# Delta rule and FFN in one kernel: chunks of 64 tokens over four batches in step, with block inverses on VectorE

## The chip, the cores and the metric

The kernel runs on one core of one Trainium2 chip. The metric is device time in microseconds, from one launch of the whole kernel; before the change it is 1528.0 us, the median of three runs (1525.26 to 1528.27). The engines go by these names: PE is TensorE's matrix products, PEld its weight loads, DVE is VectorE, ACT is ScalarE, POOL is GpSimd, and SP is the engine whose queue issues most of the DMAs.

## The reference

Two blocks follow each other. The first is a delta rule over 768 tokens for each of 4 batches and 8 heads, with a head size of 48. For each head a state of 48 x 48 is kept:

```python
k_n = k / (norm(k) + 1e-06)
for t in range(S):
    y[t]  = q[t] @ state
    v_old = k_n[t] @ state
    state = state + beta[t] * outer(k_n[t], v[t] - v_old)
```

The heads' outputs, side by side, make x with 3072 rows of 384. The second block is an FFN in which two products are multiplied with each other:

```python
a = x @ w1            # 384 -> 1024
b = x @ w2            # 384 -> 1024
out = (a * b @ w3) @ w_out   # 1024 -> 1024 -> 384
```

The weights come in float64, the rest in float32.

## The kernel before

Within a chunk of C tokens the delta rule is a triangular system. With S the state before the chunk and A strictly lower, A[t, s] = beta_s (k_t . k_s), the kernel solves (I + A) Z = V - K S, and then y = Q S + tril(Q K^T diag(beta), -1) Z and S' = S + (beta K)^T Z.

Chunks have 128 tokens of one batch. There are 24 steps, 6 chunks for each of 4 batches, and two batches alternate, so that the steps of one pair of batches are done before those of the other. For each step, `scores` does what does not wait for the state: TensorE transposes keys and queries (L261), multiplies them (L275), VectorE applies beta and the triangle (L283), and then the inverses of the diagonal blocks of 32 rows are built by doubling the block size from 2 to 32. Each doubling masks A on POOL (L295), and runs two or three groups of four products with all heads of the group on 128 x 128 (L304), with a copy on ACT (L323) and subtractions on VectorE (L328) between them. `chain` is what the state goes through: V - K S (L366, L371), Z by the block inverse (L375), three passes that settle the blocks below the diagonal (L379, L382), the output (L388, L393), the new state (L401, L415), and transposes of y so that features are on partitions (L426).

The FFN works on 384 tokens of a batch at a time. w3 and w_out are multiplied with each other once (`fold`, L505), so that it has three products per token block: two into a and b (`ab`, L449), and one with the folded weight (`o`, L463). Weights are loaded as float64 words and rounded to float32 by seven VectorE operations and one on POOL (`load_weight`, L145 to L168).

The order of the work is the order in which instructions are written, for each engine by itself. `together` (L512) takes turns between the chain of step i and the scores of step i+1, and after every second turn it emits one unit of the list `units`: first weights, then the parts of the FFN as their tokens come ready. DMAs are issued by SP in the order of the program (a DMA that has to wait holds those behind it), and the output by ACT.

Of the kernel before, what the change touches and what calls it, by code (L numbers as in the profile page):

```python
# [8 lines left out]
FP32 = mybir.dt.float32  # L9
U32 = mybir.dt.uint32  # L10
ALU = mybir.AluOpType
AX = mybir.AxisListType
# [12 lines left out]
# The FFN is ((x w1) * (x w2)) (w3 w_out): nothing stands between w3 and w_out.  # L25
# [3 lines left out]
def kernel(  # L29
# [14 lines left out]
    P = 128  # L44
    C = 128
    BS = 32
    LEVELS = [4, 8, 16, 32]
    DM = H * D
    DF = moe_w3.shape[0]
    BH = B * H  # L50
    NP = H // 2
    NCH = S // C
    KM = DM // P
    KF = DF // P
    CT = 3
    NT = CT * C
    assert S % NT == 0 and NT == DM and D == 48 and H == 8 and B % 2 == 0 and LEVELS[-1] == BS
# [3 lines left out]
    stage = ctx.enter_context(tc.tile_pool(name="stage", bufs=3))  # L61
# [3 lines left out]
    psW = ctx.enter_context(tc.tile_pool(name="psW", bufs=5, space=bass.MemoryType.PSUM))  # L65
    psY = ctx.enter_context(tc.tile_pool(name="psY", bufs=1, space=bass.MemoryType.PSUM))
    psF = ctx.enter_context(tc.tile_pool(name="psF", bufs=2, space=bass.MemoryType.PSUM))

    def bank(pool, tag):
        return pool.tile([P, 512], FP32, tag=tag, name=f"ps_{tag}")  # L70

    def quad(ps):
        return ps.rearrange("p (x w) -> p x w", x=4)

# [1 line left out]
    ident = const.tile([P, P], FP32, name="ident")  # L76
    make_identity(nc, ident[:])
    strict = const.tile([P, P], FP32, name="strict")
# [4 lines left out]
    )  # L83

    def same_block(n):
        t = work.tile([P, P // n, n], FP32, tag="same", name=f"same{n}")
        nc.gpsimd.memset(t[:], 1.0)
        nc.gpsimd.affine_select(
            out=t[:], in_=t[:], pattern=[[-n, P // n], [0, n]], compare_op=ALU.is_ge,
            fill=0.0, base=0, channel_multiplier=1,  # L90
        )
        nc.gpsimd.affine_select(
            out=t[:], in_=t[:], pattern=[[n, P // n], [0, n]], compare_op=ALU.is_ge,
            fill=0.0, base=n - 1, channel_multiplier=-1,
        )
        return t[:].rearrange("p a b -> p (a b)")

    masks = {}
    lower = ident[:]
    for n in [2] + LEVELS:  # L100
        upper = same_block(n)
        masks[n] = const.tile([P, P], FP32, name=f"mask{n}")
        nc.vector.tensor_tensor(out=masks[n][:], in0=upper, in1=lower, op=ALU.subtract)
        lower = upper
    masks["off"] = const.tile([P, P], FP32, name="mask_off")
    nc.vector.tensor_scalar(
        out=masks["off"][:], in0=lower, scalar1=-1.0, scalar2=1.0, op0=ALU.mult, op1=ALU.add
    )

    def four(m):  # L110
        return m[:].unsqueeze(1).to_broadcast([P, 4, P])

# [1 line left out]
    kbufs, bkbufs, qbufs = [], [], []  # L114
    for lst, nm, cnt in ((kbufs, "kb", 2), (qbufs, "qb", 2), (bkbufs, "bkb", 2)):
        for i in range(cnt):
            t = persist.tile([P, NP, 2, 64], FP32, name=f"{nm}{i}")
            nc.gpsimd.memset(t[:, :, :, D:64], 0.0)
            lst.append(t)
    states = []  # L120
    for b in range(B):
        t = persist.tile([P, NP, 2 * D], FP32, name=f"state{b}")
        nc.gpsimd.memset(t[:], 0.0)
        states.append(t)
    beta_tok = persist.tile([P, NCH, BH], FP32, name="beta_tok")

# [1 line left out]
    CW = 256  # L128

    def load_weight(dst, src):  # L130
        if src.dtype == FP32:
            nc.sync.dma_start(out=dst, in_=src)
            return
        n = src.shape[1]
        raw = stage.tile([P, CW, 2], U32, tag="raw", name="raw", bufs=2)
        nc.sync.dma_start(
            out=raw[:, 0:n].rearrange("p n w -> p (n w)"), in_=src.bitcast(U32)
        )
        lo, hi = raw[:, 0:n, 0], raw[:, 0:n, 1]
        sgn = work.tile([P, CW], U32, tag="wa", name="wa", bufs=2)  # L140
        man = work.tile([P, CW], U32, tag="wb", name="wb", bufs=2)
        s, m = sgn[:, 0:n], man[:, 0:n]
        sf, mf = s.bitcast(FP32), m.bitcast(FP32)
        # +-2^exponent: 0 below float32's normal range, infinite above it
        nc.vector.tensor_scalar(  # L145
            out=s, in0=hi, scalar1=20, scalar2=0x7FF,
            op0=ALU.logical_shift_right, op1=ALU.bitwise_and,
        )
        nc.vector.tensor_scalar(
            out=s, in0=s, scalar1=896.0, scalar2=1151.0, op0=ALU.max, op1=ALU.min  # L150
        )
        nc.vector.tensor_scalar(
            out=s, in0=s, scalar1=896.0, scalar2=8388608.0, op0=ALU.subtract, op1=ALU.mult
        )
        nc.vector.scalar_tensor_tensor(
            out=s, in0=hi, scalar=0x80000000, in1=s, op0=ALU.bitwise_and, op1=ALU.bitwise_or
        )
        # 1.mantissa
        nc.vector.tensor_scalar(
            out=m, in0=hi, scalar1=0xFFFFF, scalar2=None, op0=ALU.bitwise_and  # L160
        )
        nc.vector.tensor_scalar(
            out=mf, in0=m, scalar1=2.0**-20, scalar2=1.0, op0=ALU.mult, op1=ALU.add
        )
        nc.vector.scalar_tensor_tensor(
            out=mf, in0=lo, scalar=2.0**-52, in1=mf, op0=ALU.mult, op1=ALU.add
        )
        nc.gpsimd.tensor_tensor(out=dst, in0=mf, in1=sf, op=ALU.mult)  # L168

    w1s = const.tile([P, KM, DF], FP32, name="w1s")  # L170
    w2s = const.tile([P, KM, DF], FP32, name="w2s")
    w34 = const.tile([P, KF, DM], FP32, name="w34")

# [1 line left out]
    GN = 4  # L175
    steps = [(g * 2 + i, c) for g in range(B // 2) for c in range(NCH) for i in range(2)]
    N = len(steps)
    kfs, qfs, vfs, invs, Ps, Fs = {}, {}, {}, {}, {}, {}

    def chunk(src, i):  # L180
        b, c = steps[i]
        return src[b, :, c * C : (c + 1) * C, :].rearrange("h t d -> t h d")

    def load_k(g):
        kfs[g] = stage.tile([P, GN, H, D], FP32, tag="kf", name="kf", bufs=2)
        for j in range(GN):
            nc.sync.dma_start(out=kfs[g][:, j], in_=chunk(k, g * GN + j))

    def load_qv(i):
        for lst, nm, src in ((qfs, "qf", q), (vfs, "vf", v)):  # L190
            lst[i] = stage.tile([P, H, D], FP32, tag=nm, name=nm, bufs=3)
            nc.sync.dma_start(out=lst[i][:], in_=chunk(src, i))

# [1 line left out]
    def norms(g):  # L195
        ss = small.tile([P, GN, H], FP32, name="ss")
        for j in range(GN):
            sq = work.tile([P, H, D], FP32, name="sq", bufs=1)
            nc.vector.tensor_tensor(out=sq[:], in0=kfs[g][:, j], in1=kfs[g][:, j], op=ALU.mult)
            nc.vector.tensor_reduce(out=ss[:, j, :], in_=sq[:], axis=AX.X, op=ALU.add)  # L200
        seed = small.tile([P, GN, H], U32, name="seed")
        nc.vector.tensor_scalar(
            out=seed[:], in0=ss[:].bitcast(U32), scalar1=-0.5, scalar2=1597463007.0,
            op0=ALU.mult, op1=ALU.add,
        )
        r = seed[:].bitcast(FP32)
        for _ in range(3):
            t = small.tile([P, GN, H], FP32, name="nt", bufs=3)
            nc.vector.scalar_tensor_tensor(
                out=t[:], in0=ss[:], scalar=-0.5, in1=r, op0=ALU.mult, op1=ALU.mult  # L210
            )
            nc.vector.tensor_tensor(out=t[:], in0=t[:], in1=r, op=ALU.mult)
            rn = small.tile([P, GN, H], FP32, name="nr", bufs=3)
# [377 lines left out]
```

## Time and profile before

| what | before |
|---|---|
| median of three runs | 1528.0 us (1525.26 to 1528.27) |
| span of the profiled execution | 1523.8 us |
| instructions in it | 23891 |
| PE busy | 1442.6 us, 95% |
| DVE busy | 670.2 us, 44% |
| POOL busy | 546.6 us, 36% |
| ACT busy | 269.6 us, 18% |
| moved by DMA | 38.33 MB, 25 GB/s over the span |
| mean granted TensorE clock | 0.970 |

The span is from the first to the last instruction of one profiled execution; it lies 4.2 us under the median of the timed runs. "Busy" is the time in which an engine had an instruction under way. Matrix products are pipelined, so a busy PE is not a PE at its peak. A row of a group reads: line, engine, operation, what is written from what, shapes, count, then busy microseconds and the mean nanoseconds of one, and after the second bar the idle time just before them with what ended it. A row of the timeline reads: start, length, engine, line, operation, count. A row of a stretch reads: the stretch, its length, then busy time and count for PE, PEld, DVE, ACT and POOL, then the granted clock (1 is full), the busy share of the 16 DMA engines, and GB/s. An issue row ends with the kilobytes of one DMA and the microseconds from its issue to its landing.

### The profile page before, as it was taken

Reading aid. Unit: us, or ns where it says so; the run is one execution under the profiler, and the core shown is the slowest. Engines: PE = TensorE matmul, PEld = TensorE weight load, DVE = VectorE, ACT = ScalarE, POOL = GpSimd, SP = SyncE. Lnnn points to the kernel's source line nnn. Section 1 sums busy time; section 2 is a strip of 40 time slices with the busy share of each in tenths; the row PEclk is TensorE's granted clock in tenths of the full one; section 3 lists DMA queues with packets and bytes.
Section 4 is the critical chain, followed back from the end, with each engine's and each line's share of the span. In section 5 each row is a group of like instructions: output and inputs, shape, how many; then the busy total and the mean of one; then the engine's idle time right before and its main releaser. Section 6 shows DMA issues by size and latency. Waiting matters only on the chain.

```text
span 1523.8 us, 23891 instructions
## 1 busy us (share of the span) xinstructions
PE 1442.6 (95%) x9966; PEld 1246.7 (82%) x9966; DVE 670.2 (44%) x1422; ACT 269.6 (18%) x513; POOL 546.6 (36%) x489
## 2 busy tenths in 40 slices
PE   4888979999999989999999999999999999999999
PEld 3886868999988878888888888888888898889755
DVE  7998967886323343233263233332333232332100
ACT  1121202112211211121112112111121111111111
POOL 7655454655243142241342331431431422413000
PEclk8898989988999989999999999999999999999999
DMA  5221212220000000000010000000000000000000
GB/s 106 74 66 63 85 48 78 59 67 25 12 1 11 18 25 17 1 11 16 11 27 11 12 22 12 1 12 16 11 6 1 17 12 1 1 6 11 1 16 16
DMA packets 88907, 38.33 MB, mean 25 GB/s; under 512 B 76448, under 2 KB 81632, under 8 KB 88800
## 3 DMA queue, kind: packets, MB, share of 16 engines
q1 hardware_dynamic: 85248, 31.99, 8.5%
q10 hardware_dynamic: 3552, 4.82, 0.9%
q8 instruction: 79, 1.29, 0.4%
q14 instruction: 28, 0.23, 0.1%
HBM read 32.08 MB, written 4.72 MB: 24 GB/s over the span
## 4 chain that ended last, share of the span: by engine, by line
PE 74%; POOL 12%; DVE 10%; issue 1%; DMA 1%; ACT 0%; POOLq 0%; DVEq 0%
PE ps_w L304 28%; PE ps_w L352 15%; PE ps_f L449 13%; PE ps_f L463 6%; POOL M L295 6%; POOL W L312 3%; DVE AQ L283 3%; POOL offoff L295 3%; PE ps_y L393 3%; PE ps_f L505 2%; PE ps_w L275 2%; PE ps_w L261 1%; PE ps_w L401 1%; PE ps_w L366 1%; DMA raw<-in_moe_w_dram 1%
## 5 line engine op out<-in xcount | busy, mean ns | idle before, releaser
L295 POOL TENSOR_TENSOR M<-AQ,mask 128x512 f32<-128x512 f32 x240 | 313.8, 1326 | 526.4 <-PE ps_w L304 429.2
L304 PE MATMUL ps_w<-T,M 128*128 128x128 f32 x1536 | 211.3, 292 | 18.7 <-POOL M L295 15.3
L304 PEld LDWEIGHTS ps_w<-T,M 128*128 128x128 f32 x1536 | 194.2, 204 | 23.1 <-POOL M L295 19.3
L304 PE MATMUL ps_w<-W,X 128*128 128x128 f32 x1536 | 202.3, 277 | 0.0
L456 DVE TENSOR_TENSOR ab<-a,ps_f 128x384 f32<-128x384 f32 x64 | 35.5, 554 | 355.1 <-PE ps_f L449 355.1
L304 PEld LDWEIGHTS ps_w<-W,X 128*128 128x128 f32 x1536 | 186.5, 193 | 0.8
L328 DVE TENSOR_TENSOR W<-W,ps_w 128x512 f32<-128x512 f32 x192 | 131.6, 685 | 71.2 <-PE ps_w L304 71.0
L352 PE MATMUL ps_w<-E,W 128*128 128x48 f32 x1152 | 144.8, 281 | 16.4 <-DVE E L379 16.4
L304 PE MATMUL ps_w<-X,W 128*128 128x128 f32 x1152 | 159.0, 282 | 0.0
L352 PEld LDWEIGHTS ps_w<-E,W 128*128 128x128 f32 x1152 | 143.3, 202 | 18.2 <-DVE E L379 17.1
L352 PEld LDWEIGHTS ps_w<-Z,offoff 128*128 128x128 f32 x1152 | 142.4, 195 | 17.0 <-issue 1.3
L304 PEld LDWEIGHTS ps_w<-X,W 128*128 128x128 f32 x1152 | 143.3, 196 | 0.0
L352 PE MATMUL ps_w<-Z,offoff 128*128 128x48 f32 x1152 | 139.1, 274 | 0.0
L449 PE MATMUL ps_f<-xT,w1s 128*128 128x384 f32 x384 | 137.0, 491 | 0.0
L323 ACT COPY X<-ps_w 128x512 f32<-128x512 f32 x192 | 112.6, 587 | 136.3 <-PE ps_w L304 136.3
L449 PE MATMUL ps_f<-xT,w2s 128*128 128x384 f32 x384 | 134.3, 486 | 0.0
L382 ACT COPY Z<-ps_w 128x384 f32<-128x384 f32 x72 | 34.5, 479 | 559.0 <-PE ps_w L352 559.0
L463 PE MATMUL ps_f<-w,ab 128*128 128x384 f32 x384 | 128.6, 490 | 0.0
L328 DVE TENSOR_TENSOR T<-T,ps_w 128x512 f32<-128x512 f32 x144 | 98.8, 686 | 50.5 <-PE ps_w L304 47.7
L449 PEld LDWEIGHTS ps_f<-xT,w2s 128*128 128x128 f32 x384 | 73.0, 190 | 50.9
L463 PEld LDWEIGHTS ps_f<-w,ab 128*128 128x128 f32 x384 | 72.1, 192 | 48.3 <-issue 2.5
L379 DVE TENSOR_TENSOR E<-R,ps_w 128x384 f32<-128x384 f32 x60 | 33.1, 552 | 158.5 <-PE ps_w L352 158.5
(91 smaller groups left out, 1495.4 us busy)
## 6 DMA issues: line engine op xcount, KB each, us to landing
raw<-in_moe_w_dram SPq DMA_DIRECT2D x56, 256.0 KB, 3.1
kf<-in_k_dram SPq DMA_DIRECT2D x24, 192.0 KB, 3.8
qf<-in_q_dram SPq DMA_DIRECT2D x24, 192.0 KB, 3.2
vf<-in_v_dram SPq DMA_DIRECT2D x24, 192.0 KB, 2.7
out_dram<-osb ACTq DMA_DIRECT2D x24, 192.0 KB, 1.8
raw<-in_moe_w_out_dram SPq DMA_DIRECT2D x16, 192.0 KB, 2.3
beta_fm<-in_beta_dram ACTq DMA_DIRECT2D x2, 48.0 KB, 3.2
```

Of the source, the lines that this page charges most:

```text
L283: nc.vector.scalar_tensor_tensor(out=AQ[:, 2 * e + pp], in0=ps[:, 256 * pp : 256 * pp + 256].rearrange("p (j w) -> p j w", j=2), scalar=be ...
L295: nc.gpsimd.tensor_tensor(out=t[:], in0=AT, in1=four(masks[n]), op=ALU.mult)
L304: nc.tensor.matmul(quad(ps)[:, x, :], lhsT=lhs[:, x, :], rhs=rhs[:, x, :], start=True, stop=True)
L312: nc.gpsimd.tensor_tensor(out=W[:], in0=four(ident), in1=M[:], op=ALU.subtract)
L323: nc.scalar.copy(out=X[:], in_=ps)
L328: nc.vector.tensor_tensor(out=t[:], in0=t[:], in1=ps, op=ALU.subtract)
L352: nc.tensor.matmul(ps[:, D * h : D * h + D], lhsT=of_head(tiles, h), rhs=Z[:, D * h : D * h + D], start=True, stop=True,)
L382: nc.scalar.copy(out=Z[:], in_=per_head(F["W"], E))
L393: nc.tensor.matmul(py[:, D * h : D * h + D], lhsT=of_head(F["AQ"], h)[:, 1, :], rhs=Z[:, D * h : D * h + D], start=(c == 0), stop=True, sk ...
L449: nc.tensor.matmul(ps[:, 0:NT], lhsT=w[:, m, js], rhs=cur["x"][:, m, :], start=(m == 0), stop=(m == KM - 1),)
L456: nc.vector.tensor_tensor(out=cur["ab"][jc][:], in0=a[:], in1=pair[1][:, 0:NT], op=ALU.mult)
L463: nc.tensor.matmul(ps[:, 0:DM], lhsT=cur["ab"][jc][:, ts * P : (ts + 1) * P], rhs=w34[:, jc, :], start=(jc == 0), stop=(jc == KF - 1),)
```

## The change

The delta rule and its staging are written anew; the FFN keeps its products. A is kept without beta and without normalised keys: with n the norms of the keys and w = beta / n^2, the solution is scaled instead of the operands.

- A chunk has 64 tokens, and all four batches go through a chunk together: two batches lie on partitions 0 to 63 and 64 to 127 (index z), two such pairs lie side by side (index r). There are 12 chunks. Products use 64-row and 64-column parts of TensorE's array, one for each z.
- Keys and queries are loaded a second time, in blocks of 32 tokens by 32 features (`load_perm`, 32 DMAs per chunk), so that VectorE's transpose of 32 x 32 blocks brings features onto partitions (`prep`).
- The diagonal blocks of 32 rows of two chunks (128 blocks) are written to DRAM and read back with one block per partition (`to_blocks`, `inverse`). VectorE inverts all 128 at once, row by row: 31 times a product and a subtraction. They go back by DRAM into their places (`from_blocks`).
- `corner` makes the one block below the diagonal blocks out of two products, so that the whole inverse of 64 rows is there and `chain` needs one product by it, with no passes.
- `chain` gets y with features on partitions straight out of the products; ACT copies it into the FFN's input, and six small DMAs fill the remaining rows. The FFN works on 512 tokens at a time (two chunks of four batches).
- `load_weight` rounds 512 columns at a time with two operations on ACT, two on VectorE and one on POOL.
- The order is written out: per chunk `chain`, then the next chunk's `corner`, then on even chunks the preparation and the inverse of the two chunks after, then six units.

Of the diff, the lines of the new functions; what they replace is in the kernel above, and the norms, the fold and the masks change in small ways only:

```diff
-    C = 128
+    C = 64
     BS = 32
...
+    psW = ctx.enter_context(tc.tile_pool(name="psW", bufs=2, space=bass.MemoryType.PSUM))
+    psT = ctx.enter_context(tc.tile_pool(name="psT", bufs=1, space=bass.MemoryType.PSUM))
+    psF = ctx.enter_context(tc.tile_pool(name="psF", bufs=3, space=bass.MemoryType.PSUM))
...
+    def load_tok(m, dma):
+        ktoks[m] = work.tile([P, NR, H, D], FP32, tag="ktok", name="ktok", bufs=3)
+        for r in range(NR):
+            for z in range(2):
+                dma(
+                    out=ktoks[m][half(z), r],
+                    in_=k[2 * r + z, :, C * m : C * m + C, :].rearrange("h t d -> t h d"),
+                )
...
+    def load_perm(m, r, dma):
+        for src, dst in ((k, kperms[r]), (q, qperms[r])):
+            for z in range(2):
+                for j in range(2):
+                    nd = min(BS, D - BS * j)
+                    for tb in range(2):
+                        t0 = C * m + BS * tb
+                        dma(
+                            out=dst[quarter(2 * z + j), :, tb, 0:nd],
+                            in_=src[2 * r + z, :, t0 : t0 + BS, BS * j : BS * j + nd].rearrange(
+                                "h t d -> t h d"
+                            ),
+                        )
...
+    def prep(m):
...
+        for r in range(NR):
+            KQ = work.tile([P, H, 2, C], FP32, tag="KQ", name="KQ", bufs=6)
+            KQs[m, r] = KQ
+            for i, src in enumerate((kperms[r], qperms[r])):
+                nc.vector.transpose(out=KQ[:, :, i, :], in_=src[:].rearrange("p h b d -> p h (b d)"))
+            ps = two_banks()
+            for h in range(H):
+                for z in range(2):
+                    nc.tensor.matmul(
+                        ps[half(z), h // 4, 128 * (h % 4) : 128 * (h % 4) + 128],
+                        lhsT=KQ[feat(z), h, 0, :],
+                        rhs=KQ[feat(z), h].rearrange("p j t -> p (j t)"),
+                        start=True, stop=True,
+                    )
+            psv = ps[:].rearrange("p a (h j t) -> p (a h) j t", h=4, j=2)
+            nc.vector.tensor_tensor(
+                out=U[:, r], in0=psv[:, :, 0, :],
+                in1=w[:, r].unsqueeze(2).to_broadcast([P, H, C]), op=ALU.mult,
+            )
+            nc.vector.tensor_tensor(
+                out=PT[:, r], in0=psv[:, :, 1, :],
+                in1=smask[:].unsqueeze(1).to_broadcast([P, H, C]), op=ALU.mult,
+            )
...
+    def inverse(j, dma):
+        U = work.tile([P, BS, BS], FP32, tag="Ub", name="Ub", bufs=1)
+        dma(out=U[:], in_=Uds.pop(j)[:])
...
+        for s in range(BS - 1):
+            n = BS - 1 - s
+            t = work.tile([P, 256], FP32, tag="tb", name="tb", bufs=2)
+            tv = t[:, 0 : (s + 1) * n].rearrange("p (r t) -> p r t", t=n)
+            nc.vector.tensor_tensor(
+                out=tv, in0=V[:, 0 : s + 1, s : s + 1].to_broadcast([P, s + 1, n]),
+                in1=U[:, s, s + 1 : BS].unsqueeze(1).to_broadcast([P, s + 1, n]), op=ALU.mult,
+            )
+            o = V[:, 0 : s + 1, s + 1 : BS]
+            nc.vector.tensor_tensor(out=o, in0=o, in1=tv, op=ALU.subtract)
+        Vds[j] = dram.tile([P, BS, BS], FP32, tag="Vd", name="Vd")
+        dma(out=Vds[j][:], in_=V[:])
...
+    def chain(c):
...
+        def products(lhs, rhs, rows):
+            ps = two_banks()
+            for r in range(NR):
+                for h in range(H):
+                    for z in range(2):
+                        o = ps[(half if rows == C else feat)(z), r, D * h : D * h + D]
+                        nc.tensor.matmul(o, lhsT=lhs(r, h, z), rhs=rhs(r, h, z), start=True, stop=True)
+            return ps[:, :, 0:DM].rearrange("p r (h d) -> p r h d", h=H)
...
+            ps = products(
+                lambda r, h, z: KQ[r][feat(z), h, 0, :], lambda r, h, z: St[feat(z), r, h, :], C
+            )
+            nc.vector.tensor_tensor(out=R[:], in0=nv[:], in1=ps, op=ALU.subtract)
+        ps = products(
+            lambda r, h, z: TT[half(z), r, h, :], lambda r, h, z: R[half(z), r, h, :], C
+        )
...
+        raw = ffn.tile([P, CW, 2], U32, tag="raw", name="raw", bufs=2)
...
+        nc.scalar.activation(out=dst, in_=hi.bitcast(FP32), func=ACTF.Abs, scale=2.0**-112)
+        nc.scalar.activation(out=lo, in_=lo, func=ACTF.Copy, scale=2.0**-29)
...
+    emit(10)
...
+    def ahead(j):
+        for m in (2 * j, 2 * j + 1):
+            load_tok(m, sp)
+        norms(j)
+        for m in (2 * j, 2 * j + 1):
+            for r in range(NR):
+                load_perm(m, r, sp)
+            prep(m)
+            to_blocks(m, sp)
+
+    for c in range(NCH):
+        chain(c)
+        if c + 1 < NCH:
+            load_v(c + 1, sp)
+            from_blocks(c + 1, sp)
+            corner(c + 1)
+        if c % 2 == 0 and c + 2 < NCH:
+            ahead(c // 2 + 1)
+            inverse(c // 2 + 1, sp)
+        if c % 2 == 1:
+            units += ffn_units(c // 2)
+        emit(12 if c < 1 else 6)
+    emit(len(units))
```

More of the change, by code (lines that the diff above doesn't have):

```diff
@@ L98 @@
[L98 to L111, printed above, removed]
@@ L114 @@
[L114 to L125, printed above, removed]
@@ L170 @@
[L170 to L201, printed above, removed]
+    smask = const.tile([P, C], FP32, name="smask")
@@ new lines, with norms @@
+    beta_tok = const.tile([P, NCH, NR, H], FP32, name="beta_tok")
+    ns, ws = {}, {}
+    def norms(j):
+        ss = small.tile([P, 2, NR, H], FP32, name="ss")
+        for cc in range(2):
+            kt = ktoks[2 * j + cc]
+            for r in range(NR):
+                sq = work.tile([P, H, D], FP32, name="sq", bufs=1)
+                nc.gpsimd.tensor_tensor(out=sq[:], in0=kt[:, r], in1=kt[:, r], op=ALU.mult)
+                nc.vector.tensor_reduce(out=ss[:, cc, r], in_=sq[:], axis=AX.X, op=ALU.add)
+        seed = small.tile([P, 2, NR, H], U32, name="seed")
@@ L433, in slab @@
-    def slab(name):
-        return ffn.tile([P, NT], FP32, tag="ab", name=name, bufs=12)
-    def ffn_units(b, t):
-        res = []
+            ps = products(
+                lambda r, h, z: kt[half(z), r, h, :], lambda r, h, z: X[half(z), r, h, :], D
+            )
+            Sn = work.tile([P, NR, H, D], FP32, tag="S", name="S", bufs=2)
+            Ss[c + 1] = Sn
+            for z in range(2):
+                f = feat(z)
+                if c == 0:
+                    nc.vector.tensor_copy(out=Sn[f], in_=ps[f])
+                else:
+                    nc.vector.tensor_tensor(out=Sn[f], in0=St[f], in1=ps[f], op=ALU.add)
@@ L545 @@
+    prep(1)
+    to_blocks(1, act)
+    load_v(0, sp)
+    inverse(0, sp)
+    from_blocks(0, sp)
+    corner(0)
+    units = [lambda j=j: load_wo(j) for j in range(KF)]
     units += [lambda jc=jc: fold(jc) for jc in range(KF)]
     units += [lambda m=m, n0=n0: load_w12(m, n0) for n0 in range(0, DF, CW) for m in range(KM)]
-    for i in range(N):
-        if i + 2 < N:
-            load_qv(i + 2)
-        if (i + 2) % GN == 0 and i + 2 < N:
-            norms((i + 2) // GN)
-            if (i + 2) // GN + 1 < N // GN:
-                load_k((i + 2) // GN + 1)
-        runs = [chain(i)]
-        if i + 1 < N:
-            prep(i + 1)
-            runs += [scores(i + 1, 0), scores(i + 1, 1)]
-        together(runs, 4)
```

576 lines of the change are left out of this document (248 added, 328 removed).

## The prediction

> **What bounds the kernel now.** I read the page first: shares, 40 slices, chain.
>
> ```profile
> span 1523.8 us, 23891 instructions
> PE 1442.6 (95%) x9966; PEld 1246.7 (82%) x9966; DVE 670.2 (44%) x1422; ACT 269.6 (18%) x513; POOL 546.6 (36%) x489
> PE   4888979999999989999999999999999999999999
> PEclk8898989988999989999999999999999999999999
> PE 74%; POOL 12%; DVE 10%; issue 1%; DMA 1%; ACT 0%; POOLq 0%; DVEq 0%
> ```
>
> TensorE is busy nearly throughout and holds 74% of the chain that ended last; the waits for POOL's masks and VectorE are 22% of it. The first eight slices (300 us), where the weights are converted, are looser. The groups of instructions and a table by stretch say what it is busy with:
>
> ```profile
> L304 PE MATMUL ps_w<-T,M 128*128 128x128 f32 x1536 | 211.3, 292 | 18.7 <-POOL M L295 15.3 <-DVE T L328 2.2 <-POOL wo L168 0.6
> L352 PE MATMUL ps_w<-E,W 128*128 128x48 f32 x1152 | 144.8, 281 | 16.4 <-DVE E L379 16.4
> ```
> ```profile
> 606.50:664.60 58.10, 56.75 (x414) 49.70 (x413) 19.25 (x35) 10.96 (x21) 19.86 (x19) 1.00 0.04 8
> ```
>
> Each product is two instructions, call them pieces: 24 steps x 2 x 4 levels x 4 heads are 768 products of T and M, and x1536 is shown. One step (128 tokens of one batch) takes 58.1 us, so 64 tokens of four batches take 116 us. What a piece costs, from the timeline:
>
> ```profile
> 716.31 2.10 PE L275 MATMUL ps_w<-KQ 64*128 64x256 f32 x16
> ...
> 735.36 1.88 PE L352 MATMUL ps_w<-Z,offoff 128*128 128x48 f32 x16
> ...
> 1504.81 15.64 PE L463 MATMUL ps_f<-w,ab 128*128 128x384 f32 x48
> ```
>
> Each row is a start, a length and a count, so a length over a count is the spacing. A 384-column piece takes 15.64/48 = 0.32 us (its last one's drain taken off), 0.84 ns a column. Pieces of 48 columns behind 128 columns of weights take 1.88/16 = 117 ns, so there the loading of weights sets the spacing, not the 48 columns. L275 uses 64-row halves: 16 x 256 x 0.84 ns would be 3.4 us one after another, it took 2.10, so the halves ran in step.
>
> **The change, part by part.** The block inverses and the passes over Z leave TensorE: L304, L315, L352 and their like. With transposes and state products the delta part has 8616 pieces; at 0.115 us that is 990 us of the 1443. The FFN stays: 288 products of 512 columns and 192 of 384 give 576 x 0.43 + 384 x 0.32 = 371 us, as now. New delta products: 256 for each of 12 chunks, less 96 at the ends, 5952 pieces.
>
> *Price p of a small piece (32 to 64 columns on parts of the array).* No row has one. Floor: 64 x 0.84 / 2 = 27 ns, halves fully in step. Ceiling: L352's 117. One half alone: 54 + 10 = 64. L275 is the nearest row, and its halves overlap, which speaks for the floor; it shows no spacing under 100 ns, which speaks against trusting it. I take 45, about the middle of 27 and 64. The 128-column pieces of `prep` take 54 in step, 107 alone.
>
> VectorE and the queues now stand on the path, so these rows matter:
>
> ```profile
> L328 DVE TENSOR_TENSOR W<-W,ps_w 128x512 f32<-128x512 f32 x192 | 131.6, 685 | 71.2 <-PE ps_w L304 71.0
> L379 DVE TENSOR_TENSOR E<-R,ps_w 128x384 f32<-128x384 f32 x60 | 33.1, 552 | 158.5 <-PE ps_w L352 158.5
> L234 POOL TENSOR_TENSOR kb<-kf,inv 128x384 f32<-128x384 f32 x24 | 20.9, 869 | 152.4 <-issue 120.7 <-PE ps_w L261 31.0 <-POOL w2s L168 0.8
> L200 DVE TENSOR_REDUCE ss<-sq 128x8 f32<-128x384 f32 x24 | 13.2, 549 | 0.5
> ```
> ```profile
> 11.42 0.18 DVE L212 TENSOR_TENSOR nt<-nt,nr 128x32 f32<-128x32 f32 x1
> 11.64 0.19 DVE L214 SCALAR_TENSOR_TENSOR nr<-nt,nr 128x32 f32<-128x32 f32 x1
> 11.86 0.19 DVE L209 SCALAR_TENSOR_TENSOR nt<-ss,nr 128x32 f32<-128x32 f32 x1
> ```
>
> A VectorE element costs (685 - 552)/128 = 1.04 ns; dependent 32-element operations start 0.22 us apart, so each carries 0.19. *`inverse`*: 31 rows x 2 operations over 10,912 elements: 62 x 0.19 + 11.3 = 23 us for two chunks (all in one row of L328's kind: 62 x 0.69 = 43; without the fixed part: 11). A VectorE transpose of 512 has no row: 0.6, between 0.2 and 1.3.
>
> ```profile
> 656.00 0.37 SPq L192 DMA_DIRECT2D vf<-in_v_dram  x1
> ...
> 773.08 2.54 SPq L187 DMA_DIRECT2D kf<-in_k_dram  x4
> ```
> ```profile
> vf<-in_v_dram SPq DMA_DIRECT2D x8, 192.0 KB, 2.6
> ```
>
> A DMA occupies the queue 0.37 us, 0.64 when several follow; it lands in 2.6. One chunk now issues 4 + 4 for tokens and values, 32 for keys and queries in blocks of 32, 4 + 4 round trip through DRAM, nearly all on SP and in order.
>
> *Even chunk (c = 2 to 8), from its first piece, us.* The products with the keys, the inverse and for the state are 192 pieces x 0.045, with VectorE's R (768 elements, 1.25 with the waits) and X (0.85) between them: the state products end at 10.7. Only then is the buffer of keys free for chunk c+3: SP waits there, and the 32 block loads stand behind it. 36 x 0.37 + 2.6: at 26.6 the last lands (norms, 4.1 + 0.87 + 0.55 + 17 x 0.22, are ready at 20). Transposes 1.2, 64 pieces 3.5, U 0.7: 32. SP waits for U, stores it (1.5), then issues 32 loads for chunk c+3 (11.8 + 2.6): 48; transposes, pieces, U: 53.4. Store 4.1, load 3.0, inverse 23: 83.5. TensorE had 41 us of work in that time (chain 16.6, corner 7.2, preps 7, two `ab` 10.2); the `ab` products wait on VectorE behind the inverse (to 84.9), then four `o`: 20.6. Total 105.5, of which 44 idle.
>
> *Odd chunk.* Chain 16.6. ACT's copies of the features (seven of 256 elements after the last product, 0.4 each, since L323's 512 take 0.59) hold SP, which waits for them; then it issues 6 + 4 + 4 DMAs (5.2), the last lands 2.6 later, VectorE transposes (0.6): `corner` waits 11.2 in all. Corner 7.2, six `ab` of 5.1: 66. A pair of chunks is 171 where 232 stood.
>
> Here the chain is 320 pieces at 45 ns and 2.1 us of VectorE, and `corner` 128 pieces and two ACT copies of L323's kind (1.4 with the wait). I cost at nothing what POOL does: values scaled (2 x 0.87 a chunk) and squares; values land a chunk early, so the scaling runs beside the chunk before; without that cover it is 1.7 a chunk, 21 in all. VectorE's transposes take the place of TensorE's (L261) and of ACT copies, which were not on the path.
>
> ```profile
> 10.00:20.00 10.00, 4.88 (x26) 3.80 (x26) 7.22 (x23) 1.77 (x4) 8.62 (x18) 1.00 1.01 217
> ```
> ```profile
> L323 ACT COPY X<-ps_w 128x512 f32<-128x512 f32 x192 | 112.6, 587 | 136.3 <-PE ps_w L304 136.3
> L165 DVE SCALAR_TENSOR_TENSOR wb<-raw,wb 128x256 f32<-128x256 uint32 x56 | 27.4, 490 | 0.0
> L145 DVE TENSOR_SCALAR wa<-raw 128x256 uint32<-128x256 uint32 x56 | 23.7, 423 | 22.4 <-POOL w L168 12.7 <-DMA raw<-in_moe_w_dram 7.8 <-POOL w2s L168 1.9
> ...
> L295 POOL TENSOR_TENSOR M<-AQ,mask 128x512 f32<-128x512 f32 x240 | 313.8, 1326 | 526.4 <-PE ps_w L304 429.2 <-DVE AQ L283 97.2
> ```
> ```profile
> raw<-in_moe_w_dram SPq DMA_DIRECT2D x56, 256.0 KB, 3.1
> ```
>
> *Weights.* 36 loads of 512 columns. Landing 3.1 + 256 KB more at 217 GB/s, 4.4; ACT 0.59, VectorE 0.5 for the shift (L145 had 0.42 for 256, some of it waiting) and 0.75 for the sign (L165's 0.49 + 256 x 1.04 ns), POOL 1.33 like L295: 3.2 in a row; two raw buffers: 3.8 us a load, at least 2.4 (the 217 GB/s), at most 7.6. *Start.* 24 DMAs on ACT x 0.64 + 2.6: 19; norms 24; two preps with the DMAs between, 48; store, load, inverse, store, load: 85. Twelve weight loads from 81, and chunk 0's X stands behind them on VectorE: 127. Chunk 0's state ends at 134; by the even chunk's working the next inverse ends 72 later, 206. SP is held by its store until then, and 24 weight loads follow: 297.
>
> *Clock.*
>
> ```profile
> 21.00:25.00 4.00, 1.11 (x4) 0.71 (x4) 2.02 (x5) 0.00 (x0) 4.00 (x4) 0.57 0.00 0
> ...
> 60.00:70.00 10.00, 6.70 (x42) 6.34 (x41) 7.85 (x13) 0.32 (x1) 9.45 (x8) 0.80 0.32 68
> 70.00:100.00 30.00, 30.00 (x258) 29.97 (x257) 28.72 (x78) 6.77 (x13) 15.37 (x15) 0.95 0.21 58
> ```
> ```profile
> 66.16 3.49 PE L352 MATMUL ps_w<-E,W 128*128 128x48 f32 x16
> ```
>
> Where TensorE waits, the granted clock falls (0.57), and L352's sixteen take 3.49 for 1.88 until it returns. [...]
>
> **Sum.** 297 + chunk 1 without its first product 62 + 4 x 171 + chunk 10 (no inverse) 55 + chunk 11 (no corner, features landing) 52 + last units 33 = 1183; clock 44: 1227 against the span of 1523.8. The timed median of 1528.0 lies 4 above that span: 1230.
>
> **Rivals.**
> *Parts one after another.* With p = 64, 3800 pieces on the path give +72, the preps +35: 1335. For: small operands never ran in this trace. Against: L275.
> [...]
> *The edit doesn't do what it says.* The piece keeps L352's price, 117: 72 x 3800 ns = 274, preps 35: 1540, slower than before; decides from p = 114.
> *The small DMAs bound.* If a DMA of 64 or 128 byte rows costs 0.74 on SP, an even chunk gains 22, an odd 5, the start 30: 1390. For: 40 of them stand in a row in each chunk. Against: 1024-row DMAs took 0.37.
> [...]
> *The clock bounds (slower).* If TensorE, idle over a third of the time, stays at 0.5, pieces cost 171 more, preps 35, FFN 371: up to 1760, over 1528 once half of its work runs at 0.5. For: 0.57 and 0.80 above. Against: 0.95 as soon as it is fed.
> *Fewer waits.* p at 27 (-68) and half of the clock loss (-22): 1140.
>
> **Chances.** Forecast 0.44; fewer waits 0.20; one after another 0.14; small DMAs 0.10; clock 0.08; no gain per piece 0.04. Range 1070 (weights at 2.4 us a load: -50, on top of fewer waits) to 1450 (small DMAs with p = 64, or a third of the clock rival). Under 0.2% is no difference here: faster 0.87, same 0.02, slower 0.11.
>
> **What would show it.** Right: TensorE about 60% busy, 5952 small pieces at 30 to 64 ns, a 62-operation VectorE stretch of about 23 us after every even chunk's preps with TensorE waiting in `o`, SP waits at the key loads, chunk 1 at about 300. Wrong: VectorE's inverse far from 23, TensorE never waiting for it, DMAs above 0.4 us, clock under 0.8 within the FFN.

## The result, and the profile after

The changed kernel takes 836.2 us, the median of four runs (833.04 to 843.50), where the kernel before took 1526.6 beside it: a ratio of 0.548, with a 95% interval of 0.5455 to 0.5509. The prediction of 1230 had the direction, but the time lies 394 us under it and 234 under the low end of its range.

The page of the changed kernel, its span, busy shares, the 40 slices of TensorE and its clock, and the chain that ended last:

```profile
span 834.6 us, 16954 instructions
PE 649.6 (78%) x7116; PEld 401.2 (48%) x7116; DVE 359.6 (43%) x780; ACT 150.5 (18%) x305; POOL 97.6 (12%) x112
PE   0514666775718999799995998968989889996998
PEclk9756675987857989899998899997999979996999
PE 57%; DVE 13%; DMA 10%; SPq 5%; POOL 3%; issue 3%; ACT 2%; POOLq 0%; DVEq 0%; ACTq 0%
```

TensorE's busy time falls from 1442.6 to 649.6 us. The first 12 slices (250 us) are loose, and from the 13th on it is nearly full. A table by stretch (length, busy time and count of PE, PEld, DVE, ACT and POOL, clock, DMA share, GB/s) shows the two parts; the third row runs from the first `X` (L331) of chunk 2 to that of chunk 4, which is one pair of chunks:

```profile
0.00:106.00 106.00, 37.90 (x370) 29.44 (x372) 57.92 (x132) 18.69 (x33) 29.16 (x42) 0.71 0.58 115
106.00:260.00 154.00, 94.88 (x953) 63.28 (x952) 80.81 (x161) 44.82 (x82) 39.11 (x34) 0.74 0.49 113
284.40:391.80 107.40, 97.99 (x1189) 59.37 (x1190) 51.37 (x118) 16.32 (x36) 7.97 (x10) 0.92 0.34 63
```

A pair takes 107 us, where the forecast had 171 and 8 for the clock (its 44, over five and a half pairs), and the kernel before needed 232. TensorE idles 9 us of it, not 55. The groups of instructions (out of and into what, count, busy us, mean ns, idle before) say what the work costs now:

```profile
L458 PE MATMUL ps_f<-xT,w1s 128*128 128x512 f32 x288 | 152.7, 665 | 27.7 <-DMA xT<-xT 25.8
L458 PE MATMUL ps_f<-xT,w2s 128*128 128x512 f32 x288 | 137.7, 610 | 26.2 <-ACT a L465 18.7
L473 PE MATMUL ps_f<-w,ab 128*128 128x384 f32 x384 | 125.1, 487 | 0.0
L361 PE MATMUL ps_w<-PT,X 64*48 64x64 f32 x768 | 25.7, 226 | 0.5 <-DVE X L331 0.5
L245 DVE TENSOR_TENSOR tb<-Vb,Ub 128x31 f32<-128x31 f32 (+15 forms) x186 | 73.3, 394 | 17.4 <-DMA Ub<-Ud 12.3
L250 DVE TENSOR_TENSOR Vb<-Vb,tb 128x31 f32<-128x31 f32 (+15 forms) x186 | 71.2, 383 | 5.2
```

The row of L473 decides. These are the products of `o`, which need all eight `ab`; the forecast had them wait in every even chunk, to 84.9 us after its first piece, because VectorE would do `ab` after the inverse. Their idle time is 0.0. The timeline of TensorE and that of VectorE in one such place show why:

```profile
418.00 20.80 PE L473 MATMUL ps_f<-w,ab 128*128 128x384 f32 x64
438.73 2.07 PE L314 MATMUL ps_w<-S,KQ 48*64 48x48 f32 x64
441.86 2.07 PE L314 MATMUL ps_w<-R,TT 64*64 64x48 f32 x64 [1.06 <-DVE R L325]
```
```profile
434.86 0.42 DVE L245 TENSOR_TENSOR tb<-Vb,Ub 128x247 f32<-128x247 f32 x1
440.85 0.95 DVE L325 TENSOR_TENSOR R<-vtok,ps_w 128x768 f32<-128x768 f32 x1 [5.57 <-PE ps_w L314]
441.72 0.41 DVE L250 TENSOR_TENSOR Vb<-Vb,tb 128x247 f32<-128x247 f32 x1
...
443.48 0.40 DVE L250 TENSOR_TENSOR Vb<-Vb,tb 128x231 f32<-128x231 f32 x1
443.97 0.56 DVE L331 TENSOR_TENSOR X<-ps_w,w 128x384 f32<-128x384 f32 x1
444.44 0.38 DVE L245 TENSOR_TENSOR tb<-Vb,Ub 128x220 f32<-128x220 f32 x1
```

While VectorE does the rows of the inverse, TensorE has 20.8 us of `o` to do; and when the chain of the next chunk comes, its `R` (L325) and `X` (L331) stand between two rows of the inverse. In the program the whole of `inverse` is written ahead of them. So the engines do not work in the order in which the program is written, and the sentence in the description of the kernel above that says they do is wrong. Their instructions stand in another order, which the switch of the first experiment turns off (446 us more); what makes that order is called the planner from here on. VectorE keeps to it even where that costs time: at 435.28 it stops the inverse for 5.57 us, although the subtraction at 441.72 lacks nothing (the product that it takes ended at 435.28), and first does `R` at 440.85, which had to wait for TensorE.

### The profile page after: what moved, and what is told of

It reads as the page before. It is cut to its first block, busy times and chain, and to the rows that moved or that the text cites. A ratio compares the mean times of both kernels' runs of the same rounds, so it can differ in the third digit from the quotient of the medians.

```text
span 834.6 us, 16954 instructions
## 1 busy us (share of the span) xinstructions
PE 649.6 (78%) x7116; PEld 401.2 (48%) x7116; DVE 359.6 (43%) x780; ACT 150.5 (18%) x305; POOL 97.6 (12%) x112
## 4 chain that ended last, share of the span: by engine, by line
PE 57%; DVE 13%; DMA 10%; SPq 5%; POOL 3%; issue 3%; ACT 2%; POOLq 0%; DVEq 0%; ACTq 0%
PE ps_f L458 27%; PE ps_f L473 15%; PE ps_w L314 6%; DVE tb L245 3%; DMA raw<-in_moe_w_dram 3%; DVE Vb L250 3%; PE ps_w L205 3%; DMA ktok<-in_k_dram 2%; PE ps_t L274 2%; POOL w L406 2%; PE ps_f L440 2%; SPq L139 1%; DMA xT<-xT 1%; DMA kperm<-in_k_dram 1%; PE ps_t L286 1%
## 5 line engine op out<-in xcount | busy, mean ns | idle before, releaser
L458 PE MATMUL ps_f<-xT,w1s 128*128 128x512 f32 x288 | 152.7, 665 | 27.7 <-DMA xT<-xT 25.8
L458 PE MATMUL ps_f<-xT,w2s 128*128 128x512 f32 x288 | 137.7, 610 | 26.2 <-ACT a L465 18.7
L473 PE MATMUL ps_f<-w,ab 128*128 128x384 f32 x384 | 125.1, 487 | 0.0
L468 DVE TENSOR_TENSOR ab<-a,ps_f 128x512 f32<-128x512 f32 x48 | 32.9, 686 | 204.9 <-PE ps_f L458 202.9
L458 PEld LDWEIGHTS ps_f<-xT,w1s 128*128 128x128 f32 x288 | 58.0, 209 | 97.5 <-issue 92.3
L458 PEld LDWEIGHTS ps_f<-xT,w2s 128*128 128x128 f32 x288 | 55.7, 197 | 98.2 <-issue 67.7
L205 PE MATMUL ps_w<-KQ 48*64 48x128 f32 x768 | 59.6, 321 | 50.1 <-DVE KQ L201 32.5
L473 PEld LDWEIGHTS ps_f<-w,ab 128*128 128x128 f32 x384 | 72.9, 190 | 52.0 <-issue 3.0
L205 PEld LDWEIGHTS ps_w<-KQ 48*64 48x64 f32 x768 | 55.0, 164 | 56.1 <-issue 33.6
L245 DVE TENSOR_TENSOR tb<-Vb,Ub 128x31 f32<-128x31 f32 (+15 forms) x186 | 73.3, 394 | 17.4 <-DMA Ub<-Ud 12.3
L250 DVE TENSOR_TENSOR Vb<-Vb,tb 128x31 f32<-128x31 f32 (+15 forms) x186 | 71.2, 383 | 5.2
L434 PE MATMUL ps_f<-ident,w 128*128 128x128 f32 x64 | 13.8, 355 | 53.6 <-POOL w L406 53.6
L440 PE MATMUL ps_f<-wo,w3T 128*128 128x384 f32 x128 | 52.5, 573 | 0.0
L373 ACT COPY xT<-ps_w 48x256 f32<-48x256 f32 x96 | 30.5, 365 | 68.9 <-PE ps_w L361 68.4
L434 PEld LDWEIGHTS ps_f<-ident,w 128*128 128x128 f32 x64 | 9.6, 179 | 57.9 <-POOL w L406 56.1
L406 POOL TENSOR_TENSOR w<-w,raw 128x512 uint32<-128x512 uint32 x16 | 20.8, 1300 | 76.4 <-DVE w L403 42.4
```

What stands on the lines that cost most here:

```text
L205: nc.tensor.matmul(ps[half(z), h // 4, 128 * (h % 4) : 128 * (h % 4) + 128], lhsT=KQ[feat(z), h, 0, :], rhs=KQ[feat(z), h].rearrange("p j ...
L245: nc.vector.tensor_tensor(out=tv, in0=V[:, 0 : s + 1, s : s + 1].to_broadcast([P, s + 1, n]), in1=U[:, s, s + 1 : BS].unsqueeze(1).to_broa ...
L250: nc.vector.tensor_tensor(out=o, in0=o, in1=tv, op=ALU.subtract)
L373: nc.scalar.copy(out=xT[f, :, 2 * r + z, cc, :], in_=pyv[f, z, r])
L406: nc.gpsimd.tensor_tensor(out=au, in0=au, in1=lo, op=ALU.add)
L434: nc.tensor.transpose(ps[:, x, :], w3[:, x * P : (x + 1) * P], ident[:])
```

## The experiments

The theory after the result was: the prediction priced the work about right, and put it in the wrong order. Its rivals: the pieces are so much cheaper that the order matters little, or the inverse and the DMAs cost less than forecast.

### The whole kernel in the written order

Around the call of the kernel, a switch that holds all engines to the written order:

```diff
-        tile_deltanet__then__multiplicative_ffn_kernel(tc, *args)
+        with tc.manual_schedule():
+            tile_deltanet__then__multiplicative_ffn_kernel(tc, *args)
```

> Every engine issues its instructions in the order in which the program writes them; the computation is the same. In the changed kernel's trace VectorE's inverse (62 operations, 31 us with other operations between them) runs beside the chain and the FFN of the odd chunk, and weights are converted from 20 us on, which is not the order as written. Theory A (the prediction failed because it took the written order for the order on the engines): the waits worked out there come back, with the measured 31 ns a small piece 1120 to 1230 us. Theory B (the order matters little; the prices of pieces, DMAs and weights were too high): under 900 us.

Measured: 1282.5 us (1276.5 to 1289.4), 0.840 of the kernel before (0.8363 to 0.8446), above the 1120 to 1230 of theory A and far from theory B. With the same number of operations on each engine it takes 446 us longer. The stretch of a pair of chunks, from `X` to `X` as above, and then the longest waits of the whole run, TensorE's and those of SP's queue (engine and line, what it waited for, us in all, times, longest):

```profile
636.60:808.70 172.10, 105.26 (x1185) 67.29 (x1184) 52.73 (x117) 16.32 (x36) 7.55 (x10) 0.75 0.20 37
```
```profile
PE ps_w L205 <- DVE KQ L201: 166.8, 24, 13.3
PE ps_f L434 <- POOL w L406: 118.6, 16, 39.7
PE ps_t L274 <- DVE T L265: 103.0, 7, 37.7
PE ps_f L473 <- DVE ab L468: 63.6, 4, 16.6
```
```profile
SPq L480 <- ACT osb L478: 221.4, 24, 68.2
SPq L118 <- PE ps_w L314: 178.1, 5, 40.4
SPq L252 <- DVE Vb L250: 158.0, 6, 26.5
```

A pair takes 172 us, and among the waits are those that the prediction listed: SP at the key buffers (L118) and at the store of the inverted blocks (L252), `prep` behind its loads (L205), `o` behind `ab` (L473), the first product of `corner` behind the blocks (L274), the fold behind the weights (L434). SP's longest, L480, is the store of the output, of which the working said nothing. So the working of the prediction describes this kernel, and not the one that was timed. Its sizes are less good than the 172 beside 171 and 8 looks: in the pair above TensorE is busy for 105 us where 116 and 8 were forecast, and idle for 67 where 55 were, and the two misses nearly cancel.

### One engine at a time in the written order

The same switch for VectorE alone, for SP alone, and for TensorE alone:

```diff
+        with tc.manual_schedule(engines={_mybir.EngineType.DVE}):
```

> Only VectorE is held to the written order, the other engines are planned as in the changed kernel. Theory A, and the inverse standing in front of the FFN's products and of the chain's R is most of it: 980 to 1100 us. Theory A, but it is SP's queue that makes the waits: 840 to 900. Theory B: 830 to 860.

> Only SP's queue is held to the written order. If SP's order makes the waits (key and query loads behind the release of the key buffer and behind the store of U, blocks behind the features' DMAs, weights behind the store of the inverse): 950 to 1080 us. If VectorE's order makes them: 840 to 900. Theory B: 830 to 860.

> TensorE alone held to the written order, every other engine free. Theory A (TensorE's written order puts products that wait, a weight's or a preparation's, ahead of products that could run, and that is the larger part of the loss of the wholly written order): 1100 to 1280 us. Theory B (the loss comes from VectorE's and SP's order, as the 1132 and 1073 us of these two alone suggest, and TensorE only follows): under 950 us.

| held to the written order | us | above 836 |
|---|---|---|
| none | 836.2 | |
| TensorE | 895.7 (892.1 to 896.2) | 60 |
| SP | 1072.8 (1072.3 to 1073.2) | 237 |
| VectorE | 1132.2 (1125.9 to 1138.6) | 296 |
| all | 1282.5 | 446 |

TensorE's longest waits, first with VectorE held, then with SP held:

```profile
PE ps_f L473 <- DVE ab L468: 114.9, 4, 30.0
```
```profile
PE ps_f L458 <- DMA xT<-xT: 164.1, 6, 41.0
```

With VectorE held, 32 us above the 1100 that was expected at most, `o` waits four times 29 us for `ab`, which is the wait that the prediction had put into every even chunk. With SP held, the six DMAs that complete the FFN's input (L380) stand behind a store that waits for the inverse, and the FFN's first products wait for them (27 us each time; 25.8 us in all in the changed kernel). Each of the two alone costs more than half of the whole, so they overlap: what waits for one would also wait for the other. TensorE's own order is worth the least. ScalarE and GpSimd were not held alone.

### The kernel before in the written order

> The kernel before, with every engine held to the order in which its instructions are written. Theory A (the order of the engines was not the written one there either; the written turns of chain and scores are only a start): slower than 1527 us by more than 2%, 1560 to 1700 us. Theory B (there the written order was the order of the engines, so that its gain belongs to the change): 1527 us within 1%.

Measured: 1647.1 us (1644.3 to 1647.2), 1.075 of the kernel before (1.0719 to 1.0788). Theory A: the planner was at work there too, and gave 114 us. This splits the gain. In the written order the change brings 0.8405 / 1.0753 = 0.782. The planner brings 1 / 1.0753 = 0.930 to the kernel before and 0.5482 / 0.8405 = 0.652 to the changed one. TensorE's busy share suggests why it had less to give before (no run tests this by itself):

```profile
PE 1474.6 (90%) x9966; PEld 1262.2 (77%) x9966; DVE 674.6 (41%) x1422; ACT 270.3 (16%) x513; POOL 515.7 (31%) x489
```

In the written order TensorE was already busy for 90% of the time; the changed kernel in the written order has it busy for 55% (703.2 of 1279.8 us), and idle time is what another order can fill.

### Without the inverse

The loop over the rows does one of its 31 rows, so that nearly all of the inverse is left out, once in the planner's order and once in the written one:

```diff
-        for s in range(BS - 1):
+        for s in range(1):
```

> The inverse computes 1 of its 31 rows; the other 60 VectorE operations of each of the six inverses are left out, 23 us of VectorE for a pair of chunks. Theory A (the engines' order puts other work between the rows, so that the inverse lies beside TensorE's work; only the first one, ahead of chunk 0, is on the path): 805 to 836 us, and X to X of a pair of chunks stays at 103 to 109 us. Theory B (the inverse still stands on the path of every even chunk, as the prediction had it): six times 23 us less, about 700 us, X to X about 83 us.

> All engines held to the written order, and the inverse computes 1 of its 31 rows (30 rows, 23 us of VectorE for a pair of chunks, are left out). Theory A (the prediction's account holds for the written order: the inverse stands on the path of every even chunk): X to X of a pair falls from 172 to 145 to 152 us, and the time from 1282 to 1130 to 1160 us, six times 23 us less. Theory B (in the written order something else, such as SP's wait for key buffers, ends last, and the inverse is hidden there too): over 1230 us.

Measured: 807.7 us in the planner's order (805.4 to 810.2), 28 under the changed kernel, and 1165.6 in the written order (1160.2 to 1166.8), 117 under the 1282.5. A pair of chunks in the first, the same two chunks of the changed kernel (its chunks 3 to 5, `X` to `X`), and a pair in the written order:

```profile
326.20:428.90 102.70, 94.12 (x1184) 57.84 (x1184) 30.54 (x59) 16.35 (x36) 8.55 (x11) 0.95 0.37 71
```
```profile
340.60:444.00 103.40, 94.67 (x1184) 57.35 (x1184) 63.19 (x148) 16.32 (x36) 7.97 (x10) 0.95 0.36 66
```
```profile
510.30:665.30 155.00, 103.75 (x1184) 66.53 (x1184) 31.98 (x58) 16.32 (x36) 7.55 (x10) 0.76 0.22 41
```

In the planner's order 33 us less of VectorE's work in that stretch save 0.7 us: the inverse is hidden there. Half of the 28 us comes from the start (`X` of chunk 3 at 326.2, not 340.6), where chunk 0 has little to run beside it, the rest from the three later pairs, 4 to 7 us in each, so that there it is hidden for the most part only. In the written order a pair falls from 172 to 155 (145 to 152 were expected), and the time by 117, a little less than the 122 to 152 expected: most of the 24 us of each inverse is on the path there. The prediction's account of the inverse holds for the order that it assumed.

### The price of a small piece

In `prep`, `corner` and `chain` the two halves (z) take turns product by product (a product is two pieces). Here the loop over z goes outside those over heads (and, but in `prep`, over r) wherever such products are issued; one of these loops:

```diff
-            for r in range(NR):
-                for h in range(H):
-                    for z in range(2):
+            for z in range(2):
+                for r in range(NR):
+                    for h in range(H):
```

> The two 64-row halves take turns by groups of 8 to 16 products (32 to 64 instructions) and not product by product; nothing else changes. If the price of 31 ns a piece comes from the halves running in step and needs neighbours in the order: up to 60 ns a piece on 5952 pieces, +170 us at most, 920 to 1010. If TensorE takes instructions of both halves out of its queue whatever their order (as the kernel before showed with groups of four), or if the price is set by something else: 830 to 870, and 64 pieces still span about 2.0 us.

Measured: 1031.9 us (1031.6 to 1032.1), 196 more than the changed kernel and above the 920 to 1010 that were expected. The 64 pieces that apply the inverse, at two places of this run, and 200 us in the steady part, first of this run and then of the changed kernel:

```profile
456.15 3.73 PE L314 MATMUL ps_w<-R,TT 64*64 64x48 f32 x64
...
533.20 6.14 PE L314 MATMUL ps_w<-R,TT 64*64 64x48 f32 x64 [1.05 <-DVE R L325]
```
```profile
400.00:600.00 200.00, 190.81 (x1627) 133.56 (x1626) 79.34 (x180) 24.74 (x54) 10.61 (x14) 0.78 0.27 48
```
```profile
400.00:600.00 200.00, 175.61 (x1974) 106.06 (x1971) 98.67 (x227) 28.44 (x62) 15.62 (x20) 0.93 0.36 66
```

Sixty-four pieces take 3.73 or 6.14 us where they took 2.07 (the row at 441.86 above). The stretches of little but these pieces, the two of this run and then that of the changed kernel, say how much of it is the clock (third figure from the end):

```profile
456.15:459.88 3.73, 3.73 (x67) 3.68 (x67) 0.69 (x1) 0.00 (x0) 0.00 (x0) 1.00 0.00 0
533.20:539.34 6.14, 6.13 (x64) 5.97 (x64) 1.88 (x5) 0.00 (x0) 1.66 (x2) 0.55 0.35 67
```
```profile
441.86:443.95 2.09, 2.06 (x64) 1.94 (x64) 1.88 (x5) 0.00 (x0) 0.00 (x0) 1.00 0.27 55
```

At the full clock a piece thus takes 58 ns by halves and 32 in turns. The 96 ns of the other row come with a granted clock of 0.55. So the low price of a short piece came here only with a neighbour in the order that is on the other half of the array. By an estimate from these rows, 26 ns on the 5184 pieces outside `prep` are 135 of the 196 us; how the rest divides between the pieces of `prep` and the lower clock (0.79 over this run, 0.87 over the changed kernel) was not taken apart.

### The start

In the changed kernel TensorE is busy for 28.6 us of the 60 from 200 to 260, and SP's timeline there has the blocks of chunks 2 and 3 (L256) behind 48 weight DMAs:

```profile
199.15 0.34 SPq L252 DMA_DIRECT2D Vd<-Vb  x1
199.61 52.84 SPq L392 DMA_DIRECT2D raw<-in_moe_w_dram  x48
252.49 4.31 SPq L256 DMA_DIRECT2D TT<-Vd  x8
```

Three edits went at it: four buffers of raw weights in place of two (and of `a`, which shares them); the DMAs of L256 on ACT's queue; and, with that, four buffers each for the loads in blocks of 32.

```diff
-        raw = ffn.tile([P, CW, 2], U32, tag="raw", name="raw", bufs=2)
+        raw = ffn.tile([P, CW, 2], U32, tag="raw", name="raw", bufs=4)
...
-            from_blocks(c + 1, sp)
+            from_blocks(c + 1, act)
...
-    kperms = padded("kperm", [P, H, 2, BS], 2)
+    kperms = padded("kperm", [P, H, 2, BS], 4)
```

> Four buffers for raw weights in place of two. In the changed kernel SP waits 87 us in the first 260 for conversions to free a buffer (46.6 + 18.2 + 12.4 + 5.7 + 4.1). Theory A (two buffers set the pace of the weights, and the weights set when the FFN can begin): weights done at about 200 in place of 258, 790 to 820 us. Theory B (the time under the weights is spent on the chain and preparations anyway, TensorE has all its work to do after them): within 1% of 836 us.

> The four DMAs that bring a chunk's inverted blocks into place go out on ACT's queue; only those of chunk 0 stay on SP's. In the changed kernel those of chunks 2 and 3 stand behind 48 weight DMAs on SP (52.84 us, from 199.61 on), and X of chunk 2 is at 284. Theory A (TensorE lacks work at 200 to 260, 28.6 busy of 60, because of that queue): X of chunk 2 at 210 to 240, and 795 to 825 us. Theory B (the weights end the wait anyway, the FFN's products come after them in any case): within 1% of 836 us, X of chunk 2 earlier with no gain behind it.

> As the run with the blocks' DMAs on ACT's queue, and four buffers each for keys and queries in blocks of 32 in place of two, one pair for each of two chunks, so that SP need not wait for a chunk's transposes before it loads the next chunk's. Theory A (the release of these buffers delays the first inverse, which starts at 56.4, and the later ones): the first inverse starts 8 to 15 us earlier, and the time is 8 to 20 us below that of the run with the blocks' DMAs on ACT's queue alone. Theory B (hidden behind other work): within 5 us of it.

Measured: 839.6 (835.1 to 841.4), 832.3 (830.2 to 833.9) and 832.4 us (829.9 to 835.2). None is told apart from the changed kernel with certainty: the ratios to the kernel before are 0.5479 (0.5455 to 0.5504), 0.5443 (0.5426 to 0.5461) and 0.5445 (0.5424 to 0.5467), beside 0.5482 (0.5455 to 0.5509). So theory B in each. With L256 on ACT's queue `X` of chunk 2 does come earlier, at 227.0 and not 284.4, but `X` of chunk 3 only moves from 340.6 to 338.5, and the stretches from 200 to 260 and, by the same view, from 260 to 300 have TensorE busy for 35.3 and 31.4 us in place of 28.6 and 39.3: work was moved ahead and was missing after. With four raw buffers the weights end 7 us earlier (252.1, not 259.0), with nothing gained. With four block buffers the first inverse starts at 56.6 and not at 56.4, where theory A had 8 to 15 us earlier. What does set the time of the start was not settled by these runs; the queue and the raw buffers were each excluded as the one cause, and so were the block buffers together with the queue.

## Why the prediction was wrong

**The order.** The step that failed is the one under all of the even chunk, the odd chunk and the start: that each engine takes its instructions in the order of the program. It entered with the description of the kernel, and every wait was built on it: "SP waits there, and the 32 block loads stand behind it", "the `ab` products wait on VectorE behind the inverse", "SP is held by its store until then, and 24 weight loads follow". The run in the written order has all of these waits; in the changed kernel `o` does not wait for `ab` at all (0.0, for 63.6 there), and SP's two waits, 178.1 and 158.0 there, fall to these:

```profile
SPq L118 <- PE ps_w L314: 69.4, 8, 19.1
...
SPq L252 <- DVE Vb L250: 30.2, 6, 7.6
```

What the runs put in the place of that step is an order in which other work stands between, worth 446 us. The trace of before showed it already. All copies into `beta_tok` (L539) are written ahead of the call of `norms`, whose steps are L202 to L214; VectorE's timeline of the kernel before has them mixed:

```profile
8.91 0.28 DVE L539 COPY beta_tok<-ps_f 128x32 f32<-128x32 f32 x2
9.11 0.18 DVE L209 SCALAR_TENSOR_TENSOR nt<-ss,seed 128x32 f32<-128x32 f32 x1
...
9.61 0.28 DVE L539 COPY beta_tok<-ps_f 128x32 f32<-128x32 f32 x2
9.81 0.18 DVE L212 TENSOR_TENSOR nt<-nt,seed 128x32 f32<-128x32 f32 x1
```

One such pair of rows was enough to doubt the sentence, and the run of that kernel in the written order, 114 us slower, confirms it.

**The sum, term by term.** By the prediction `X` of chunk 2 came at 297 + 62 + 8 = 367, and it came at 284.4: 83 less. Four pairs at 171 were 684, and from `X` of chunk 2 to that of chunk 10 (711.9) it took 427.5: 256 less. From there to the end 132 were forecast and 122.7 taken: 9 less. The 44 for the clock are inside the measured terms. Together 83 + 256 + 9 + 44 = 392, which is 1227 less the span of 834.6. In a pair, 171 and 8 had 116 us of TensorE's work, 55 idle and 8 of clock; measured are 98 busy and 9 idle. So of the 72 us of a pair the lost idle time is 46, and the cheaper work with the clock 26.

**Price of a piece.** It was taken at 45 ns. The rows of the pieces of 32 to 64 columns come to 155 us for 5184, 30 ns each; L361's row above is 25.7 / 768 = 33. The floor of 27 was nearer than the middle. L275 had spoken for it, and the objection that no row showed a spacing under 100 ns was no evidence, since no row had such short pieces on parts of the array. The pieces of `prep` were put at 54; in the changed kernel's stretch from 400 to 600 they take 65:

```profile
L205 PE MATMUL ps_w<-KQ 48*64 48x128 f32 x256 | 16.7, 290 | 3.6 <-DVE PT L216 3.6
```

**The rivals.** *Parts one after another* fell with 30 ns a piece. The run with z outside shows what the rival looks like when it does hold: 58 ns at the full clock, beside its 64. *No gain per piece* fell with the same number. *The small DMAs bound*: eight block loads in a row took SP 3.90 us, 0.49 each (first row below, of the run in the written order), so 0.37 was too low and 0.74 too high. That they do not bound in the planner's order is argued from the 9 us that TensorE idles in a pair; no run priced them alone. *The clock bounds* fell: 0.92 in the steady pair, although the whole kernel has 0.871. *Fewer waits* had the right direction, and its 1140 was far too cautious, since it took only half of the clock loss away and left the 55 us idle.

```profile
195.87 3.90 SPq L139 DMA_DIRECT2D qperm<-in_q_dram  x8
...
245.85 144.35 SPq L392 DMA_DIRECT2D raw<-in_moe_w_dram  x60
```

**The other terms.** *Inverse*: 23 us forecast, (73.3 + 71.2) / 6 = 24.1 measured. *Weights*: 3.8 us a load forecast; in the written order the last 24 loads took 144.35 us (second row above, of the same run), 6.0 each, which is 53 more than 24 x 3.8. The twelve of w3 are 8.2 us apart in POOL's last step (L406), those of w1 and w2 4.0: a load of w3 stands behind the fold's own transposes and copies on the same engines, which the working left out. *The FFN* was taken as 371 us; its three rows come to 152.7 + 137.7 + 125.1 = 415.5. `o` has its price (384 x 0.32 = 123), so the 44 are nearly all in L458. How much of them is the clock at the start, and how much the interleaving with small pieces, was not taken apart. *Figures without a row*: no run shows the 44 us that the sum has for the clock, 8 a pair; the runs have a clock of 0.92 in the steady pair and of 0.75 in the one of the written order. The 10 ns in the 64 of one half alone was the author's estimate (L352's 117 less 128 x 0.84 would be 9.5); a half alone took 58. A VectorE transpose of 512, put at 0.6, takes 0.70 in the changed kernel ((16.9 + 16.7) / 48, L201).

**What was right.** The work that is removed and added, the inverse, the direction, and that TensorE sets the time of the FFN stretches (0.0 us idle before the 125.1 of `o`, 53.9 before the 290.4 of the first two products). As a forecast of the kernel in the written order, 1230 is 4% low, and that it comes so near is in part luck: pieces were too dear, waits and weights too cheap. There `X` of chunk 2 comes at 465.7, 99 later than the 367, with 53 of the 99 in the weights, and the four pairs take 687, beside 684 and 32 for the clock.

## What to carry to other kernels

Before summing waits, find out which order the engines really have: look in the trace for two instructions on one engine whose order differs from the program's. If there are such, take waits from the data alone (what must be there before an instruction can start, and which engine has enough other work to cover it), and treat a wait that comes only from written order as covered as long as another engine's work is to be had (here the written order takes 446 us more). Where parts of TensorE's array are to run in step, let neighbouring products alternate between the parts (here 32 ns a piece, and 58 in groups by half).

## What the runs showed that was not expected

- Alternating halves matter: pieces of 48 columns on 64 rows sustain 32 ns (2.07 / 64), and in groups by half 58 ns (3.73 / 64), both at the full clock, for the same products in the same buffers; at a clock of 0.55 it is 96 ns (6.14 / 64).
- The granted clock does not follow TensorE's busy share alone. In the run with z outside TensorE is busy for 95% of the stretch from 400 to 600, and the clock is 0.78; in the changed kernel it is busy for 88% and the clock is 0.93. What lowers it there was not shown.
- A wait that is taken from one place can come back with the next chunk at no gain: `X` of chunk 2 was 57 us earlier with its blocks on another queue, and the time was the same to 0.5%.
